# Six buffers for the high parts of g and four for the low parts, where it was four and six

## The chip, the cores and the metric

The kernel runs on one core of one Trainium2 chip. The metric is the time of one execution on the device in microseconds (us), as the median of several runs. A profile comes from one further execution, whose own time is given beside its span.

## The reference

```python
def reference(x, w_in, w_out, w_gate, w1, w2):         # x: 8 x 3072 x 256
    X = fft(fft(x, axis=1), axis=2).real                # 24576 rows of 256
    h = X.reshape(24576, 256) @ w_in                    # 256 -> 2048
    g = h * clip(h + 3, 0, 6) / 6
    x = g @ w_out                                       # 2048 -> 256
    e = argmax(x @ w_gate, axis=1)                      # 8 experts, with the softmax weight of the best
    return weight[e] * (relu(x @ w1[e]) @ w2[e])        # rows grouped by expert
```

## The kernel before

The work has two stages. The first, up to about 2080 us of the span, makes the Fourier transform, the layer with g and the routing; the second runs the experts. The change is in the first. There the tokens of a batch are cut into six chunks of 512 columns, and each chunk is worked through in 8 steps (48 steps a batch, 384 in all), one step for each 256 of the 2048 hidden features.

For accuracy a float32 number is carried as the sum of two parts, a high one in a narrower type and a low one (the remainder), and a product is three matmuls: high with high, high with low, low with high. A step `s` of the loop `step` does this:

- TensorE: 14 matmuls into a tile `ab` of PSUM (`mm1`; called U here), which needs `ab` to be free. There are two `ab` tiles, so U of step s needs that the last reader of `ab` of step s-2 is done.
- `h_of`: ScalarE copies half of `ab` to `A` (L502), VectorE makes a difference (L189) and a sum (L186) in `ab`.
- `relu6`: ScalarE writes two tiles `r` (L508). `gate_h`: VectorE multiplies each with `ab` in place (L515). These two are called the gates here; the second frees `ab`.
- ScalarE copies the two `r` to `gh`, the high part (L962); GpSimd (POOL) subtracts, `gl = r - gh` (L189 on POOL), which also frees `r`.
- Three steps later (`LAG = 3`) TensorE multiplies both with `w_out`: 24 matmuls into `acc` (`mm2`), first 16 that read `gh`, then 8 that read `gl`. That frees `gh` and `gl`.

So `r`, `gh` and `gl` are rings, with two tiles for each step. Their depth is the table `BUFS`, which `halves` reads:

```python
    def halves(tag, dt, s):
        return [pw.tile([P, 2, 256], dt, tag=tag, bufs=BUFS[tag], name=f"{tag}{s}_{n}") for n in range(2)]
```

Between the steps stand other jobs, which are hung on numbered steps: the folds of the next batch (VectorE L186 and L194 on tiles `R` and `H`, POOL on `H`), their splits into parts (ScalarE L182, VectorE L183 on `SC0s`, `SS0s`, `SC`, `SS1s`), the Fourier matmuls (`f`, `fe`, `fo`) with `vc`, `pf` and `pq`, and at each chunk's end the evacuation of `acc` (`xo`, `xp`) and the routing (`rt_...`), with four indirect DMAs that POOL issues to write rows to DRAM (`xs`, L149).

What an engine does in which order is settled when the kernel is built: a scheduler takes instructions by priority (their order in the program) as soon as it holds their inputs to be there and a buffer of their ring to be free. After that each engine runs its own list in that order, and semaphores make it wait.

Of the kernel before, what the change touches and what calls it, by code (L numbers as in the profile page):

```python
# [43 lines left out]
EC = 5  # L44
EX = 6
RKW = 4
BUFS = dict(r=4, gh=4, gl=6)
EXTRA = 23
LATE = (0, 0, 1, 1, 2, 3, 3, 4, 5, 5, 6, 6, 7, 7, 8, 8, 8, 9)
RK = 2  # L50
# [24 lines left out]
def tile_fft_moe(ctx, tc, xr, xf, xcoef, w_in, w_out, w_gate, w1, w2, tabs, fm, misc, tri, sgn8, dstc, maskc, out):  # L75
# [435 lines left out]
    def halves(tag, dt, s):  # L511
        return [pw.tile([P, 2, 256], dt, tag=tag, bufs=BUFS[tag], name=f"{tag}{s}_{n}") for n in range(2)]

# [100 lines left out]
    if True:  # L614
# [409 lines left out]
        ge = pw.tile([P, NTILE, NE + 1], F32, tag="xp", name="ge")  # L1024
        tt = pw.tile([P, NTILE, NE], F32, tag="r", bufs=BUFS["r"], name="tt")
        dve.memset(ge[:, :, 0:1], 1.0)
# [258 lines left out]
```

## Time and profile before

| | us |
|---|---|
| median of 3 runs | 3274.42 |
| lowest and highest | 3268.84, 3277.36 |
| profiled execution, its own time | 3273.91 |
| its span | 3272.1 |

The span is what the profile covers, from the first instruction to the last; the 1.8 us beside it are outside the program's instructions. The time of an engine that counts as busy is not the time that it bounds: TensorE is busy for 95% of the span, and what it waits for is in the rows below.

### The profile page before, as it was taken

How to read it: one execution, taken by the hardware profiler on the slowest of the kernel's cores; microseconds unless marked ns; L12 is line 12 of the kernel's file. 1: busy time of each engine (PE TensorE's matmuls, PEld its weight loads, DVE VectorE, ACT ScalarE, POOL GpSimd, SP SyncE). 2: the span in 40 equal slices, each digit the busy share in tenths (PEclk: the TensorE clock that was granted, in tenths of full speed). 3: DMA queues.
4: the chain of work that ended last, by engine and by line, in shares of the span. 5: the costliest groups of instructions: out<-in, count | busy, mean ns of one | idle time of the engine just before them, and what ended most of it. 6: DMA issues, size and time to landing. Idle time of an engine off the chain costs nothing.

```text
span 3272.1 us, 61901 instructions
## 1 busy us (share of the span) xinstructions
PE 3116.5 (95%) x23482; PEld 2983.7 (91%) x23482; DVE 2117.7 (65%) x3699; ACT 1952.4 (60%) x3339; POOL 2123.1 (65%) x1784
## 2 busy tenths in 40 slices
PE   5899999999999999999999999999999999999998
PEld 5889999999999999999999999988888888888887
DVE  8586777777777777777777666755555555555553
ACT  3566666666666666667666766654444454444453
POOL 5466766766766766766766665676666566666664
PEclk8899999999999999999999999999999999999999
DMA  5100100100100100100100002274555455555550
GB/s 184 62 27 16 44 24 16 43 24 16 44 24 16 44 24 16 44 24 16 34 14 16 15 14 53 63 200 149 147 154 152 140 166 152 149 147 155 145 173 26
DMA packets 256189, 243.14 MB, mean 74 GB/s; under 512 B 157739, under 2 KB 219020, under 8 KB 255888
## 3 DMA queue, kind: packets, MB, share of 16 engines
q1 hardware_dynamic: 234640, 184.66, 20.0%
q0 software_dynamic: 21248, 54.48, 4.6%
q8 instruction: 187, 3.06, 0.4%
q14 instruction: 114, 0.93, 0.1%
HBM read 159.71 MB, written 54.04 MB: 65 GB/s over the span
## 4 chain that ended last, share of the span: by engine, by line
PE 61%; DVE 22%; ACT 10%; issue 3%; POOL 2%; DMA 1%; SPq 0%; ACTq 0%; DVEq 0%; POOLq 0%
PE op L164 16%; PE acc L164 16%; PE hp L164 15%; PE ab L164 11%; DVE r L515 6%; ACT r L508 5%; DVE ab L186 3%; DVE ab L189 3%; ACT xp L546 1%; ACT gh L962 1%; DVE H L194 1%; ACT xo L539 1%; PE wi L164 1%; DVE H L186 1%; DVE xTa L189 1%
## 5 line engine op out<-in xcount | busy, mean ns | idle before, releaser
L189 POOL TENSOR_TENSOR gl<-r,gh 128x512 fp32r<-128x512 f32 x768 | 1018.7, 1349 | 541.4 <-ACT gh L962 536.7
L164 PE MATMUL acc<-WO,gh 128*128 128x264 f32 x6144 | 831.7, 286 | 4.5 <-ACT xo L539 2.3
L515 DVE SCALAR_TENSOR_TENSOR r<-r,ab 128x512 f32<-128x512 f32 x768 | 493.0, 683 | 460.8 <-ACT r L508 452.9
L164 PEld LDWEIGHTS acc<-WO,gh 128*128 128x128 f32 x6144 | 780.9, 190 | 6.5 <-ACT WO L182 3.3
L508 ACT ACTIVATE r<-ab,half 128x512 f32<-128x512 f32 x768 | 486.2, 684 | 241.0 <-DVE ab L186 219.5
L962 ACT ACTIVATE gh<-r 128x512 fp32r<-128x512 f32 x768 | 454.5, 628 | 203.2 <-PE acc L164 145.6
L1000 DVE SCALAR_TENSOR_TENSOR WB<-hp,WA 128x512 fp32r<-128x512 f32 (+1 forms) x472 | 278.7, 607 | 299.4 <-ACT WA L999 293.8
L164 PE MATMUL ab<-pq,WA 128*128 128x256 f32 x2304 | 398.3, 289 | 69.4 <-DVE r L515 63.6
L164 PE MATMUL acc<-WO,gl 128*128 128x264 f32 x3072 | 439.9, 285 | 0.0
L164 PEld LDWEIGHTS ab<-pq,WA 128*128 128x128 f32 x2304 | 330.6, 192 | 90.0 <-issue 82.4
L164 PEld LDWEIGHTS acc<-WO,gl 128*128 128x128 f32 x3072 | 402.8, 189 | 0.0
L999 ACT ACTIVATE WA<-hp 128x512 fp32r<-128x512 f32 (+1 forms) x472 | 241.4, 531 | 194.8 <-PE hp L164 192.7
L164 PE MATMUL ab<-pq,WB 128*128 128x256 f32 x2304 | 342.3, 285 | 0.0
L502 ACT ACTIVATE A<-ab 128x512 f32<-128x512 f32 x384 | 230.1, 599 | 158.7 <-PE ab L164 138.6
L149 POOL DMA_INDIRECT out_dram<-yo,dst x200 | 217.6, 1088 | 156.5 <-DVE yo L1100 119.4
L164 PEld LDWEIGHTS ab<-pq,WB 128*128 128x128 f32 x2304 | 307.7, 193 | 0.0
L164 PE MATMUL hp<-xTb,TB 128*128 128x512 f32 (+1 forms) x1344 | 277.3, 364 | 13.7 <-DVE WB L1000 13.5
L189 DVE TENSOR_TENSOR ab<-A,ab 128x512 f32<-128x512 f32 x384 | 264.7, 689 | 32.8 <-ACT A L502 25.3
L164 PEld LDWEIGHTS hp<-xTb,TB 128*128 128x128 f32 x1344 | 225.8, 188 | 57.9 <-DVE WB L1000 15.2
L164 PE MATMUL hp<-xTa,W1b 128*128 128x512 f32 (+1 forms) x1392 | 275.6, 357 | 1.6 <-DVE WB L1000 1.6
L164 PE MATMUL op<-W2b,WA 128*128 128x256 f32 x1536 | 275.0, 281 | 0.0
L186 DVE TENSOR_TENSOR ab<-A,ab 128x512 f32<-128x512 f32 x384 | 266.8, 695 | 11.5
(269 smaller groups left out, 5300.8 us busy)
## 6 DMA issues: line engine op xcount, KB each, us to landing
w1a<-in_w_dram SPq DMA_DIRECT2D x29, 1024.0 KB
w1b<-in_w_dram SPq DMA_DIRECT2D x29, 1024.0 KB
w2b<-in_w_dram SPq DMA_DIRECT2D x58, 512.0 KB
R<-in_xr_dram SPq DMA_DIRECT2D x32, 774.0 KB
w2a<-in_w_dram SPq DMA_DIRECT2D x29, 768.0 KB
w2d<-in_w_dram SPq DMA_DIRECT2D x28, 256.0 KB
q<-pq SPq DMA_DIRECT2D x288, 1.0 KB
raw<-in_w_in_dram SPq DMA_DIRECT2D x8, 512.0 KB
```

Of the source, the lines that this page charges most:

```text
L149: i = pool.indirect_dma_start(oob_is_err=False, **kw)
L164: i = pe.matmul(*a, **kw)
L186: pinned(eng.tensor_tensor(out=o, in0=a, in1=b, op=ALU.add))
L189: i = eng.tensor_tensor(out=o, in0=a, in1=b, op=ALU.subtract)
L194: pinned(dve.scalar_tensor_tensor(out=o, in0=a, scalar=s, in1=b, op0=ALU.mult, op1=ALU.add))
L502: act.activation(A, h[0], AF.Copy)
L508: act.activation(r, h, AF.Relu, bias=half, scale=1.0 / 6.0)
L515: dve.scalar_tensor_tensor(out=g, in0=r, scalar=1.0, in1=h, op0=ALU.min, op1=ALU.mult)
L539: act.activation(xo[:, t, :], acc[t][:, 0:GW], AF.Copy)
L962: act.activation(gh[n], r[n], AF.Copy)
L999: act.activation(hi, ps, AF.Relu)
L1000: dve.scalar_tensor_tensor(out=lo, in0=ps, scalar=0.0, in1=hi, op0=ALU.max, op1=ALU.subtract)
```

## The change

The depth of two rings is exchanged. `gh` has tiles for three steps instead of two, `gl` for two instead of three. Tiles of both kinds are equally large (512 numbers of 4 bytes on each of 128 partitions), so that the memory is the same.

```diff
-BUFS = dict(r=4, gh=4, gl=6)
+BUFS = dict(r=4, gh=6, gl=4)
```

No instruction of the computation is added or removed. Two things follow for the lists of the engines. An instruction that writes `gh` of step s waits for TensorE's readers of `gh` of step s-3 instead of s-2, and one that writes `gl` of step s for the readers of `gl` of step s-2 instead of s-3. And the scheduler, which held ScalarE's `gh` back until a ring tile was free, places it earlier, and orders other instructions around it anew. From the third batch to the sixth the new order is the same in every batch.

Two places in a batch are shown. The first is POOL's list in a chunk's third step, at the place that the rows below show between 1478 and 1502 us (names with numbers are buffers of one step: `gl_0_19129` and `gl_1_19130` are the two low parts of the step whose U runs just before 1478 us).

```order
 L269 DMA sgn_18889<-in_sgn_dram 128x258
 L578 COPY rt_occ_19373<-cnt 128x8
+L189 TENSOR_TENSOR gl_0_19129<-r_0_19125,gh_0_19127 128x512
+L189 TENSOR_TENSOR gl_1_19130<-r_1_19126,gh_1_19128 128x512
 L149 DMA xs_dram<-xp_18589,pic_19162 198656x260 x3
 L581 TENSOR_TENSOR rt_occ_19373<-rt_occ_19373,rt_ohc_19309 128x8
 L149 DMA xs_dram<-xp_18589,pic_19162 198656x260
-L189 TENSOR_TENSOR gl_0_19129<-r_0_19125,gh_0_19127 128x512
-L189 TENSOR_TENSOR gl_1_19130<-r_1_19126,gh_1_19128 128x512
 L581 TENSOR_TENSOR rt_occ_19373<-rt_occ_19373,rt_ohc_19309 128x8 x2
 L581 TENSOR_TENSOR cnt<-rt_occ_19373,rt_ohc_19309 128x8
```

The two `gl` have moved from behind the four DMA issues to before them.

The second place is ScalarE's list, one chunk earlier in its batch, around 1680 us of the rows below. `r_0_21893` belongs to the step whose U ends before 1678 us, `ab_21939` and `ab_22011` are the tiles of the two steps after it (U at 1683.22 and 1686.53 us). Before:

```order
L508 ACTIVATE r_1_21894<-ab_21833,half 128x512
L539 ACTIVATE xo_21907<-acc_2_21404 128x264
L539 ACTIVATE xo_21907<-acc_3_21405 128x264
L326 ACTIVATE vc_2_0_21915<-f_2_0_21873 128x256
L546 ACTIVATE xp_21908<-xo_21907 128x4x256 x2
L182 ACTIVATE pq_2_21872<-pf_2_0_21916 128x512
L561 ACTIVATE rt_exc_22009<-rt_dc_22006 128x32
L502 ACTIVATE A_21982<-ab_21939 128x512
L962 ACTIVATE gh_0_21895<-r_0_21893 128x512
L962 ACTIVATE gh_1_21896<-r_1_21894 128x512
L508 ACTIVATE r_0_21986<-ab_21939,half 128x512
```

And after the change:

```order
L539 ACTIVATE xo_21907<-acc_3_21405 128x264
L546 ACTIVATE xp_21908<-xo_21907 128x4x256
L962 ACTIVATE gh_0_21895<-r_0_21893 128x512
L962 ACTIVATE gh_1_21896<-r_1_21894 128x512
L546 ACTIVATE xp_21908<-xo_21907 128x4x256
L326 ACTIVATE vc_2_0_21915<-f_2_0_21873 128x256
L502 ACTIVATE A_21982<-ab_21939 128x512
L561 ACTIVATE rt_exc_22009<-rt_dc_22006 128x32
L182 ACTIVATE pq_2_21872<-pf_2_0_21916 128x512
L502 ACTIVATE A_22050<-ab_22011 128x512
L508 ACTIVATE r_0_21986<-ab_21939,half 128x512
```

The two `gh` now stand between the two halves of `xp`, `vc` has moved behind both halves, and `r` of the step at 1683.22 us comes after `A` of the step at 1686.53 us.

## Rows read from the trace of the kernel before

**Rows 1.** The profile's page: busy time of the engines, share of the span, instructions.

```profile
PE 3116.5 (95%) x23482; PEld 2983.7 (91%) x23482; DVE 2117.7 (65%) x3699; ACT 1952.4 (60%) x3339; POOL 2123.1 (65%) x1784
```

**Rows 2.** Busy time by stretch: busy us (instructions) of PE, PEld, DVE, ACT, POOL; PEclk; DMA.

```profile
210.00:2080.00 1870.00, 1810.49 (x14736) 1783.68 (x14735) 1337.28 (x2486) 1279.81 (x2318) 1262.95 (x1256) 0.99 0.08 26
```

**Rows 3.** TensorE's waits from 210 to 2080 us: total, times, longest.

```profile
PE ab L164 <- DVE r L515: 56.7, 55, 2.4
```

**Rows 4.** Timeline of an undisturbed stretch: start, length, engine, [idle before, releaser].

```profile
1303.33 1.15 ACT L962 ACTIVATE gh<-r 128x512 fp32r<-128x512 f32 x2 [0.86 <-PE acc L164]
...
1303.61 1.15 PE L164 MATMUL acc<-WO,gl 128*128 128x264 f32 x8
1304.04 2.54 POOL L189 TENSOR_TENSOR gl<-r,gh 128x512 fp32r<-128x512 f32 x2 [2.02 <-ACT gh L962]
...
1308.60 2.54 POOL L189 TENSOR_TENSOR gl<-r,gh 128x512 fp32r<-128x512 f32 x2 [2.02 <-ACT gh L962]
...
1309.26 1.27 ACT L508 ACTIVATE r<-ab,half 128x512 f32<-128x512 f32 x2 [0.22 <-DVE ab L186]
```

**Rows 5.** VectorE from 1502 to 1747 us by form: count, busy us, mean ns.

```profile
L189 DVE TENSOR_TENSOR ab<-A,ab 128x512 f32<-128x512 f32 x49 | 33.7, 688 | 1.1 <-ACT A L502 0.6
...
L566 DVE SCALAR_TENSOR_TENSOR rt_kc<-rt_dc,iom 128x32 f32<-128x32 f32 x6 | 1.1, 184 | 0.0
```

**Rows 6.** Timeline from 1478 to 1502 us, TensorE, VectorE and POOL.

```profile
1488.05 0.52 PE L164 MATMUL ab<-pq,WA 128*128 128x256 f32 x3
...
1494.18 0.59 PE L164 MATMUL ab<-pq,WA 128*128 128x256 f32 x3 [1.41 <-DVE r L515]
...
1501.40 0.60 PE L164 MATMUL ab<-pq,WA 128*128 128x256 f32 x3 [2.42 <-DVE r L515]
...
1478.49 1.29 DVE L515 SCALAR_TENSOR_TENSOR r<-r,ab 128x512 f32<-128x512 f32 x2 [1.63 <-ACT r L508]
...
1482.02 0.69 DVE L183 SCALAR_TENSOR_TENSOR pq<-pf,pq 128x512 fp32r<-128x512 f32 x1
...
1485.45 1.28 DVE L515 SCALAR_TENSOR_TENSOR r<-r,ab 128x512 f32<-128x512 f32 x2 [0.56 <-issue]
1486.65 3.03 DVE L183 SCALAR_TENSOR_TENSOR SC<-H,SC 128x258 fp32r<-128x258 f32 x2
1489.61 0.42 DVE L186 TENSOR_TENSOR H<-H 128x258 f32<-128x258 f32 x1
...
1492.75 1.28 DVE L515 SCALAR_TENSOR_TENSOR r<-r,ab 128x512 f32<-128x512 f32 x2 [1.40 <-ACT r L508]
...
1481.47 1.03 POOL L149 DMA_INDIRECT xs_dram<-xp,pic  x1 [1.55 <-DVE rt_kc L566]
...
1486.49 2.56 POOL L189 TENSOR_TENSOR gl<-r,gh 128x512 fp32r<-128x512 f32 x2
```

**Rows 7.** Timeline from 1678 to 1699 us, all four engines.

```profile
1691.09 0.52 PE L164 MATMUL ab<-pq,WA 128*128 128x256 f32 x3
...
1697.74 0.59 PE L164 MATMUL ab<-pq,WA 128*128 128x256 f32 x3 [1.92 <-DVE r L515]
...
1682.43 2.05 ACT L546 ACTIVATE xp<-xo 128x1024 uint16<-128x1024 uint16 x2
...
1682.99 0.42 DVE L327 TENSOR_TENSOR pf<-f,vc 128x256 f32<-128x256 f32 x1
...
1688.82 1.28 DVE L515 SCALAR_TENSOR_TENSOR r<-r,ab 128x512 f32<-128x512 f32 x2 [1.11 <-ACT r L508]
1690.03 3.55 DVE L183 SCALAR_TENSOR_TENSOR SC0s<-H,SC0s 128x258 fp32r<-128x258 f32 x1
...
1689.45 2.55 POOL L189 TENSOR_TENSOR gl<-r,gh 128x512 fp32r<-128x512 f32 x2
...
1692.55 1.29 POOL L189 TENSOR_TENSOR H<-R 128x258 f32<-128x258 f32 x2
```

**Rows 8.** POOL's instructions that write gl: who waited for them (us, times).

```profile
  ACT r L508: 5.7, 11
```

## The prediction

> **What bounds the kernel now.** I read the page first, then the busy time of the first stage, then TensorE's waits in it, and last the places where those waits stand. The page shows TensorE busy for 95% of the span [rows 1]. From 210 to 2080 us, nearly all of the stage that the change touches, it is busy for 1810 of 1870 us at a granted clock of 0.99, while VectorE, ScalarE and POOL are each busy for some 70% [rows 2]. So a shorter wait of another engine gives nothing, unless TensorE stood behind it. It stands behind one thing in the main: 56.7 us in 55 waits of a U for VectorE's gates, that is, for an `ab` tile [rows 3]. That is the most the change can give back there, 1.7% of the time.
>
> TensorE never waits for `gh` or `gl` in these rows. What waits for the rings is ScalarE: in an undisturbed stretch `gh` waits 0.86 us until TensorE has read the `gh` of two steps before, and `gl` on POOL follows it [rows 4]. This is the wait that the change removes, and it lies beside TensorE's work: a step lasts 4.56 us there (from one `gl` to the next), and no U waits.
>
> **The change in an undisturbed step.** `gh` no longer waits, which gains nothing in the end. `gl` now waits for TensorE's readers of `gl` two steps before. These are the 8 matmuls at 1303.61; the sixth is the last that reads the first tile. At 1.15 us for eight it ends about 1304.5, where `gl` started at 1304.04 [rows 4]: `gl` comes some 0.45 us later in each step. Behind it on POOL stand folds and scatters, and ScalarE's `r` of two steps later waits for its tile. That `r` starts at 1309.26 and `gl` ended at 1304.04 + 2.54 = 1306.58, so that 2.7 us of slack become 2.2. Cost nothing, as long as POOL is not more than 2.2 us late.
>
> **The change where TensorE stands.** The waits come in a pattern that each of six batches repeats. Two places carry most of it: 1.92 us around 1698 [rows 7], and 1.41 and 2.42 us around 1494 and 1501 [rows 6]; six times 5.75 is 34.5 of the 56.7 us. In both, one thing lengthens VectorE's list ahead of the gates. At 1690.03 the low part of `SC0s` takes 3.55 us, of which 0.42 are its work (the like instruction on as many numbers at 1489.61). It ends only when POOL, which runs `gl` and then `H` without a gap from 1689.45, is past its third instruction [rows 7]. At 1486.65 the two `SC` take 3.03 us while POOL runs `gl` from 1486.49 to 1489.05 [rows 6]. VectorE instructions with two inputs in SBUF wait there for POOL's.
>
> The Trainium skill (SBUF — State Buffer, Who interferes with whom) says that a VectorE instruction with two SBUF inputs contends with a GpSimd instruction that reads SBUF, and that the one which comes first holds the ports for its whole length. The rows agree that it waits, but 3.55 us is longer than the one instruction of POOL (1.28 us, half of 2.55) that the rule lets it wait for. By the rule a collision that stays would cost 1.3 us at most, and the lower bound around 1690 below would be a gain of 0.5 instead of a loss of 0.4.
>
> The changed order moves POOL's `gl` ahead of the scatters at both places (shown for one), so that POOL issues scatters while VectorE does its splits. A scatter does not hold VectorE up: `pq`, with two SBUF inputs, took its usual 0.69 us at 1482.02 beside the scatter of 1481.47 to 1482.50 [rows 6]. Against that, ScalarE's list puts `gh` between the halves of `xp` and `vc` behind them, and VectorE's copy into `xp` and `pf` wait for both. So the gates come later before they come sooner.
>
> *Around 1690.* `xp` ended at 1682.43 + 2.05 = 1684.5; two `gh` of 1.15 us together [rows 4] put it near 1685.4 (`vc` no longer ahead of it), `vc` at 1685.8. On VectorE follow two `pf` of 0.42, then a difference and a sum for each of two steps and one `pq`, five of 0.69, some ten routing operations of 0.18 [rows 5, 7], partly overlapped (1.3 to 1.8), and the gates, 1.28: 1685.8 + 0.8 + 3.5 + 1.6 + 1.3 = 1693.0, against 1690.1 now. The U at 1691.09 has six matmuls of 0.12 us (the step has 38 in 4.56 us) moved ahead of it, so it could start at 1691.8 and waits 1.3 us, until 1693.1. The next gates need `SC0s` at 0.42 and 1.28 more, 1694.8. The U after that starts when TensorE gets there, 14 + 18 matmuls or 3.85 us on, at 1697.0 where it was 1697.74. I take a gain of 0.5 us. With `SC0s` at 3.55 again it is 1698.1, a loss of 0.4; with nothing late, 1696.4, a gain of 1.4.
>
> *Around 1494.* Here the two `gh` can start when the gates of their step end, 1479.8, and stand before both halves of `xp`: 1.15 + 2.05 + 0.4 for `vc` is 1483.3, and the same 7.2 us of VectorE's list put the first gates' end at 1490.5 where it was 1486.7 [rows 6], and the U of 1488.05 (seven matmuls ahead of it, so 1488.9) at 1490.6. But the sum and difference of the next step now stand before these gates, and the `SC` pair is beside scatters: 0.8 us instead of 3.03, `H` 0.4, gates 1.3: next gates end at 1493.0, where it was 1494.0. That U starts at 1494.4, 31 matmuls on and no longer waiting. From its gates to the next ones VectorE needed 1501.25 - 1494.03 = 7.2 us; from 1493.0 that is 1500.2 at the latest. The U of 1501.40 starts near 1500.1: a gain of 1.35. If `SC` takes 3.03 again the gates end 1495.2 and this U starts at 1502.4, a loss of 1.0; if the later pair of splits and `H` (1.5 us at 1495.73) are freed too, TensorE's own pace allows 1498.9, a gain of 2.5.
>
> **The sum.** 6 x 1.35 + 6 x 0.5 = 11.1 us. The smaller waits (56.7 - 34.5 = 22 us) and the first two hundred us, where the order changes as well, I take at nothing: the lists move both ways there, and they may give or take some 8 us. Bounds of the two places: 6 x (-1.0 - 0.4) = -8 and 6 x (2.5 + 1.4) = +23. Against the profiled execution's 3273.9 us (its span and 1.8 us beside it; 0.5 us below the median of the runs, so no correction) that gives 3262.8. About 0.3%, 10 us, is what a measurement here can tell from no change.
>
> **The rivals.**
> - *Gain given back.* The later gates at the chunk ends eat what the splits give, and the undisturbed steps stay at TensorE's pace: 3274. For it speaks that TensorE is at 1810 of 1870 us already; against it, that POOL's and VectorE's collision is 3.1 us at one place.
> - *Slower: POOL late, `r` held.* Four scatters of 1.0 us at a chunk's end put POOL behind, and `gl` may no longer run ahead of TensorE by three steps. Then `r` waits for `gl`, the gates for `r` and U for the gates. It decides when `gl` is more than 2.2 us late. Before, `r` waited so for only 5.7 us, 11 times [rows 8], which speaks against it. Price: 0.45 us at each of 48 chunk ends, 22 us, less the 11: 3285.
> - *More freed.* If the collisions go at all places, half of the 56.7 us comes back: 3273.9 - 28.3 = 3245.6. That each collision is chance speaks against it: every `gl` moves by 0.45 us against the folds `R` and `H` in each step, so that new collisions come with those that go.
>
> **How the numbers follow.** Forecast 45% (3262.8, itself 3255 to 3270; six in ten of it faster by more than 0.3%, the rest the same), given back 23% (nearly all the same), slower 18%, more freed 14%. That makes faster 0.43, same 0.36, slower 0.21. The range takes the better half of the last case and the slower one but for its tail: 3243 to 3284.
>
> **What would show it.** Right: TensorE's waits for the gates fall by about ten us; the wait at the place of 1698 is gone and one of 1 to 2 us stands a step earlier; `SC0s` there takes 0.4 us; ScalarE's `gh` hardly waits for TensorE and POOL's `gl` waits for TensorE instead of ScalarE. Wrong: `SC0s` and `SC` as long as before, or moved collisions at folds that were free; ScalarE's `r` waiting for POOL for tens of us; new waits for the gates in the third and fifth step of the chunks.

## The result and the profile after

The changed kernel takes 3296.1 us (median of 6 runs, 3292.2 to 3302.2) where the kernel before took 3274.0 beside it: a ratio of 1.0073, 95% interval 1.0061 to 1.0085, so 22 us slower. The forecast was 3262.8, 11 us faster, in a range from 3243 to 3284.

The profile's page, busy time of the engines as in [rows 1], has nothing of this: each engine does what it did before.

```profile
PE 3117.0 (95%) x23482; PEld 2983.1 (91%) x23482; DVE 2123.4 (64%) x3699; ACT 1958.9 (59%) x3339; POOL 2118.6 (64%) x1784
```

The stretch of [rows 2] again, by busy time: TensorE 1789.6 us where it was 1810.5, 21 us less work in the same time.

```profile
210.00:2080.00 1870.00, 1789.58 (x14536) 1761.10 (x14535) 1323.28 (x2454) 1267.38 (x2281) 1239.94 (x1241) 0.99 0.08 26
```

TensorE's waits in it, as in [rows 3]: the wait for the gates grew from 56.7 us to 63.4, and more stand behind the routing (`rt_kc`, 0.6 us before, and `rt_mc`) and the evacuation (`xo`), for which no wait is listed before.

```profile
PE ab L164 <- DVE r L515: 63.4, 67, 3.0
PE ab L164 <- DVE rt_kc L592: 4.5, 7, 3.3
PE acc L164 <- ACT xo L539: 4.3, 8, 1.4
PE ab L164 <- DVE rt_mc L558: 3.5, 12, 0.3
```

POOL's `gl` in the same stretch, what it waited for and, below, who waited for it, which answers to [rows 8]:

```profile
  PE acc L164: 393.8, 176
  ACT gh L962: 99.0, 59
...
  ACT r L508: 36.3, 44
```

So `gl` did change from waiting for `gh` to waiting for TensorE, and ScalarE's `r` waits for `gl` six times as long as before (36.3 us, before 5.7). That looks like the rival "POOL late, `r` held". The experiments show that it isn't.

**Where the 21 us between the two spans arise.** Each step has one `A` on ScalarE, and the starts of the first `A` of each piece, in either trace, cut the stage (us; "what follows" ends with POOL's last instruction; the runs below stand beside the two for later use):

| kernel | step 0 to 80 | five batches, 80 to 320 | 320 to 383 | what follows |
|---|---|---|---|---|
| before | 475.5 | 1228.9 | 322.7 | 1184.8 |
| changed | 471.1 | 1234.2 | 341.8 | 1185.3 |
| gl two steps, gh two | 469.4 | 1226.5 | 322.6 | 1184.9 |
| changed, gh behind A everywhere | 473.2 | 1220.1 | 328.3 | 1185.6 |
| changed, gh behind A from step 328 | 474.0 | 1233.6 | 327.9 | 1183.7 |
| changed, gh behind A at chunk ends up to 327 | 458.9 | 1204.2 | 343.9 | 1186.6 |
| both of these | 465.1 | 1203.8 | 329.3 | 1187.7 |
| gh behind A at all chunk ends, A behind gh elsewhere | 473.4 | 1235.4 | 338.3 | 1182.9 |

The start gains 4.5 us, the five batches lose 5.3, and 19.2 us are lost in the last eight chunks: 0.6 in the first of them, where the last folds and splits stand, and the rest in the seven after it, which have none. The prediction had looked at none of these chunks.

**The last chunks.** Busy time from 1800 to 1965 us, first of the kernel before:

```profile
1800.00:1965.00 165.00, 165.00 (x1362) 163.90 (x1360) 100.45 (x201) 112.24 (x203) 103.38 (x102) 0.99 0.04 14
```

and of the changed kernel:

```profile
1800.00:1965.00 165.00, 155.47 (x1264) 152.91 (x1263) 102.77 (x196) 108.41 (x196) 99.97 (x99) 0.99 0.04 14
```

TensorE was never idle there; now it does 98 matmuls fewer (11.9 us, at 0.121 us apart) and is idle for 9.5, at the same granted clock, 0.99. These 9.5 us are waits that the profile lists, 5.2 of them for the gates; the other 2.4, by difference, are starts that come a little late, as shown below. The timeline of an undisturbed step of the changed kernel, which answers to [rows 4], shows one of two causes (start, length, engine, idle before):

```profile
1837.44 0.52 PE L164 MATMUL ab<-pq,WA 128*128 128x256 f32 x3
...
1841.46 0.63 ACT L962 ACTIVATE gh<-r 128x512 fp32r<-128x512 f32 x1 [0.81 <-DVE r L515]
1842.00 0.58 ACT L502 ACTIVATE A<-ab 128x512 f32<-128x512 f32 x1
1842.11 0.59 PE L164 MATMUL ab<-pq,WA 128*128 128x256 f32 x3
1842.17 2.55 POOL L189 TENSOR_TENSOR gl<-r,gh 128x512 fp32r<-128x512 f32 x2 [2.11 <-PE acc L164]
...
1842.61 0.70 DVE L189 TENSOR_TENSOR ab<-A,ab 128x512 f32<-128x512 f32 x1 [0.65 <-ACT A L502]
1843.34 0.69 DVE L186 TENSOR_TENSOR ab<-A,ab 128x512 f32<-128x512 f32 x1
1844.13 1.27 ACT L508 ACTIVATE r<-ab,half 128x512 f32<-128x512 f32 x2 [1.03 <-DVE ab L186]
1845.43 1.28 DVE L515 SCALAR_TENSOR_TENSOR r<-r,ab 128x512 f32<-128x512 f32 x2 [1.40 <-ACT r L508]
1846.21 0.63 ACT L962 ACTIVATE gh<-r 128x512 fp32r<-128x512 f32 x1 [0.81 <-PE acc L164]
1846.75 0.58 ACT L502 ACTIVATE A<-ab 128x512 f32<-128x512 f32 x1
```

The first `gh` of a step now stands ahead of the next step's `A` in ScalarE's list. The U that writes that `A`'s input begins at 1837.44, and its 14 matmuls are over by 1839.26, but `A` starts at 1842.00, right behind `gh`. And `gh` needs the gate, the gate `r`, `r` the sum, the sum the difference and the difference the `A` before: the rows close a loop, 0.61 + 0.73 + 0.79 + 1.30 + 0.78 + 0.54 = 4.75 us from one `A` to the next, where TensorE's work takes 4.57. (For the `gh` at 1846.21 the row names TensorE. But TensorE's 16 matmuls that had to be done for it had started at 1839.10 and took 2.09 us, while the first of the two gates ended at 1846.12: it is the gate.) That ScalarE doesn't let a ready `A` pass a waiting `gh` is what the Trainium skill says (PSUM — Partial Sum Buffer, Engine vs sequencer instructions: its queue is strictly first in, first out); the rows agree, since `A` waits 2.7 us with its input there. In the kernel before, `A` of the next step stood ahead of `gh` in these steps, and no loop closed.

TensorE's share of this doesn't appear among its waits: the records of its matmuls last 0.28 us (their ends are modelled) and start every 0.12, so that a start that is late by up to 0.16 us leaves no idle time between two records. The first two matmuls of the U at 1842.11 start 0.22 and 0.19 us after the ones ahead of them, instead of 0.12.

**The chunk's end.** The place of [rows 7] in the changed kernel, 1686 to 1699 us:

```profile
1685.87 1.06 ACT L546 ACTIVATE xp<-xo 128x1024 uint16<-128x1024 uint16 x1
...
1686.84 1.14 ACT L962 ACTIVATE gh<-r 128x512 fp32r<-128x512 f32 x2
1687.02 0.60 PE L164 MATMUL ab<-pq,WA 128*128 128x256 f32 x3
1687.88 1.04 ACT L546 ACTIVATE xp<-xo 128x1024 uint16<-128x1024 uint16 x1
1688.83 0.36 ACT L326 ACTIVATE vc<-f 128x256 f32<-128x256 f32 x1
1688.95 0.17 DVE L605 COPY xp<-dst_sb 128x12 f32<-128x12 f32 x1 [1.75 <-ACT xp L546]
1690.41 2.99 POOL L189 TENSOR_TENSOR gl<-r,gh 128x512 fp32r<-128x512 f32 x2 [3.93 <-PE acc L164]
1690.68 1.57 DVE L183 SCALAR_TENSOR_TENSOR pq<-pf,pq 128x512 fp32r<-128x512 f32 x1
1692.17 1.28 DVE L595 TENSOR_TENSOR rt_kc<-rt_kc,rt_ohc 128x32 f32<-128x32 f32 x1
1693.37 0.68 DVE L186 TENSOR_TENSOR ab<-A,ab 128x512 f32<-128x512 f32 x1
1697.83 0.42 DVE L183 SCALAR_TENSOR_TENSOR SC0s<-H,SC0s 128x258 fp32r<-128x258 f32 x1
1698.06 0.59 PE L164 MATMUL ab<-pq,WA 128*128 128x256 f32 x3 [2.28 <-DVE r L515]
```

`SC0s` has its 0.42 us, as predicted. But the two `gh` between the halves of `xp` keep `vc` back, and VectorE stands with its copy into `xp` for 1.75 us. So `pq` comes just when `gl` runs: it takes 1.57 us, and `rt_kc` with its 32 numbers 1.28. The sum behind them is late, the gates too, and U waits 2.28 us. VectorE's instructions from 500 to 1755 us by form in the changed kernel (count, then busy us and mean ns) show the exchange:

```profile
L183 DVE SCALAR_TENSOR_TENSOR pq<-pf,pq 128x512 fp32r<-128x512 f32 x21 | 29.5, 1405 | 0.5
L595 DVE TENSOR_TENSOR rt_kc<-rt_kc,rt_ohc 128x32 f32<-128x32 f32 x31 | 22.8, 735 | 0.0
L183 DVE SCALAR_TENSOR_TENSOR SC<-H,SC 128x254 fp32r<-128x254 f32 x11 | 8.3, 758 | 0.0
L183 DVE SCALAR_TENSOR_TENSOR SC0s<-H,SC0s 128x258 fp32r<-128x258 f32 x11 | 7.5, 679 | 0.0
L183 DVE SCALAR_TENSOR_TENSOR SC<-H,SC 128x258 fp32r<-128x258 f32 x11 | 4.6, 421 | 0.0
L194 DVE SCALAR_TENSOR_TENSOR H<-H 128x258 f32<-128x258 f32 x11 | 4.6, 419 | 0.0
L183 DVE SCALAR_TENSOR_TENSOR SS1s<-H,SS1s 128x254 fp32r<-128x254 f32 x11 | 4.5, 413 | 0.0
```

against the kernel before:

```profile
L183 DVE SCALAR_TENSOR_TENSOR SC0s<-H,SC0s 128x258 fp32r<-128x258 f32 x11 | 20.3, 1842 | 0.0
L183 DVE SCALAR_TENSOR_TENSOR SC<-H,SC 128x258 fp32r<-128x258 f32 x11 | 15.8, 1436 | 0.0
L183 DVE SCALAR_TENSOR_TENSOR pq<-pf,pq 128x512 fp32r<-128x512 f32 x20 | 13.8, 690 | 1.2
L183 DVE SCALAR_TENSOR_TENSOR SS1s<-H,SS1s 128x254 fp32r<-128x254 f32 x11 | 11.2, 1017 | 0.0
L194 DVE SCALAR_TENSOR_TENSOR H<-H 128x258 f32<-128x258 f32 x11 | 11.2, 1014 | 0.0
L595 DVE TENSOR_TENSOR rt_kc<-rt_kc,rt_ohc 128x32 f32<-128x32 f32 x30 | 9.8, 326 | 0.0
L183 DVE SCALAR_TENSOR_TENSOR SC<-H,SC 128x254 fp32r<-128x254 f32 x11 | 6.8, 622 | 0.0
```

The splits `SC0s` and `SC` gave back 22.5 us, the split `SS1s` and the fold `H` another 13.3; `pq` and `rt_kc` took 28.7, with one instruction more of each in the window. So in sum these instructions of VectorE take no longer than before. What counts is where the time goes, and `pq` and the routing stand at the chunks' ends, ahead of gates that a U waits for.

### The profile page after: what moved, and what is told of

Its sections match the earlier page's. It is cut to its first block, busy times and chain, and to the rows that moved or that the text cites. A ratio compares the mean times of both kernels' runs of the same rounds, so it can differ in the third digit from the quotient of the medians.

```text
span 3293.3 us, 62041 instructions
## 1 busy us (share of the span) xinstructions
PE 3117.0 (95%) x23482; PEld 2983.1 (91%) x23482; DVE 2123.4 (64%) x3699; ACT 1958.9 (59%) x3339; POOL 2118.6 (64%) x1784
## 4 chain that ended last, share of the span: by engine, by line
PE 47%; DVE 28%; ACT 16%; issue 3%; POOL 3%; DMA 1%; SPq 0%; ACTq 0%; DVEq 0%; POOLq 0%
PE op L164 16%; PE hp L164 15%; PE acc L164 8%; ACT r L508 8%; DVE r L515 8%; PE ab L164 6%; DVE ab L186 5%; DVE ab L189 4%; ACT gh L962 2%; ACT xp L546 2%; POOL gl L189 1%; DVE pq L183 1%; DVE R L194 1%; DVE rt_kc L595 1%; PE wi L164 1%
## 5 line engine op out<-in xcount | busy, mean ns | idle before, releaser
L164 PE MATMUL acc<-WO,gh 128*128 128x264 f32 x6144 | 844.1, 287 | 7.2 <-ACT xo L539 6.5
L164 PEld LDWEIGHTS acc<-WO,gh 128*128 128x128 f32 x6144 | 788.9, 191 | 9.9 <-ACT xo L539 8.4
L962 ACT ACTIVATE gh<-r 128x512 fp32r<-128x512 f32 x768 | 466.8, 631 | 106.1 <-DVE r L515 103.4
L164 PE MATMUL hp<-xTb,TB 128*128 128x512 f32 (+1 forms) x1344 | 277.4, 364 | 13.3 <-DVE WB L1000 13.0
```

Source lines behind the costliest of these rows:

```text
L164: i = pe.matmul(*a, **kw)
L962: act.activation(gh[n], r[n], AF.Copy)
```

## The experiments

Theory A: the loss lies in the lists that the deeper `gh` makes the scheduler write. Theory B: it lies in the ring of `gl` that is one step shorter.

**Half of the change alone.** Only `gl` is made shorter.

```diff
-BUFS = dict(r=4, gh=4, gl=6)
+BUFS = dict(r=4, gh=4, gl=4)
```

> gh keeps its two steps, and gl goes from three to two, so half of the change: no deeper gh. The lists of TensorE, ScalarE and VectorE are then the same as before, row for row, and POOL's nearly so. Theory A (the loss lies in the new lists: ScalarE has gh of a step ahead of A of the next step, and between the halves of xp): no loss, 3274 us within 6. Theory B (the loss lies in the two-step ring of gl: POOL's gl waits for TensorE, r for gl, the gates for r): most of the loss is there, 3288 to 3297.

Measured: 3266.5 us, ratio 0.9986 (0.9976 to 0.9996). No loss, with the lists of ScalarE and VectorE the same as before, row for row. `gl` waits 310.1 us for TensorE, and ScalarE's `r` 26.0 us for `gl`, and with these lists that doesn't make the kernel slower: theory B falls. The 5 us below the kernel before are within the 0.3%.

**The rings of the change, the old place of gh.** What writes `gh` and `gl` is emitted one step later, behind the next step's `A`, with an edge that fixes the order of `A` and `gh` in ScalarE's list and makes nobody wait. The scheduler orders the rest of all lists around it anew.

```diff
                 h = h_of(ab, s)
+                if "low" in hold:
+                    hold.pop("low")(hold["A"])
...
-                for n in range(2):
-                    act.activation(gh[n], r[n], AF.Copy)
-                for n in range(2):
-                    sub(pool, gl[n], r[n], gh[n])
+                def low(after, r=r, gh=gh, gl=gl):
+                    for n in range(2):
+                        i = act.activation(gh[n], r[n], AF.Copy)
+                        tc.add_manual_dep(i.ins, after.ins.name, NOSYNC, reason="behind A")
+                    for n in range(2):
+                        sub(pool, gl[n], r[n], gh[n])
+                hold["low"] = low
```

> The changed rings (gh six tiles, gl four), but each step's gh is held behind A of the next step in ScalarE's list, as nearly all of them stood before. Theory A: the steps of the last chunks go back from 4.75 to 4.57 us and the time to 3268 to 3280. Theory B: the rings are those of the change, so 3290 to 3298.

Measured: 3263.8 us, 0.9969 (0.9958 to 0.9981): the loss is gone and 10 us beside it, with the rings of the change. `r` waits 48.2 us for `gl` in this run, more than in the changed kernel, so this wait isn't what the 22 us are.

**Both rings deep.** `xp` gives the memory (so do two other tiles that share its ring).

```diff
-BUFS = dict(r=4, gh=6, gl=4)
+BUFS = dict(r=4, gh=6, gl=6)
...
-                xp = pw.tile([P, 4, XW], I32, tag="xp", name=f"xp{z}")
+                xp = pw.tile([P, 4, XW], I32, tag="xp", bufs=1, name=f"xp{z}")
```

> gh has three steps as in the change and gl keeps its three; to make room xp has one buffer instead of two, which is what the next run has alone. Theory A: slower than the next run by 10 to 25 us, because ScalarE's list has gh ahead of A again (in the chunks 42 to 46 in 26 of 40 steps). Theory B: gl is as deep as before, so within 5 us of the next run.

And its baseline, `xp` alone:

> The rings of before, xp with one buffer instead of two: the baseline of the run with both rings deep. Both theories: 3274 within 8, if the rows are out of xp before the next chunk's end; the order changes a little, too.

Measured: 3474.1 and 3443.5 us. The second was off by 170 us for both theories: ScalarE's `xp` stands until the scatters of the `xp` before have landed, in this row of ScalarE's waits from 210 to 2080 us:

```profile
ACT xp L546 <- DMA xs_dram<-xp,pic: 149.2, 41, 5.0
```

Most of that is the order of the kernel itself. It issues the scatters of a chunk only at the next chunk's end: an `xp` written until 1519.9 us is scattered from 1557.1 to 1562.3, and the next one starts at 1564.8, after ScalarE has waited 4.0 us. A scatter takes some 2.7 us there from its issue to its landing.

The deeper `gh` costs 31 us in this pair, with `gl` as deep as it was. The sign is that of theory A, but with a baseline so changed the pair proves little.

**The place in the stage.** The edge of the second run, but only in some steps; where it isn't, `gh` is emitted as in the changed kernel. In the last chunks:

```diff
+                if s >= 328:
+                    hold["low"] = low
+                else:
+                    low(None)
```

> The changed kernel, with gh held behind A of the next step only from step 328 on (the chunks 41 to 47); up to there its lists are the changed kernel's, row for row. Theory A, with most of the loss in the last chunks (17 of 21 us by the times of A): 3276 to 3283. If the loss came from the whole stage in equal parts: 3292 to 3296.

> As the run before, but gh is held only in the steps 2 to 4 of each of those chunks, where the evacuation, xp and the routing stand. By the widths between one A and the next, a chunk of the changed kernel loses 4.0 us: 0.8 in four undisturbed steps of 4.75 instead of 4.57 us, 3.2 in the other four. Theory A1 (the chunk's end carries the loss: gh between the halves of xp, r behind two A): 12 of the 17 us come back, 3282 to 3287. Theory A2 (the loop A, difference, sum, r, gate, gh, A of the undisturbed steps makes both): 3290 to 3295.

> The complement: gh is held behind A from step 328 on in all steps but 2 to 4 of a chunk. Theory A1: only the 0.19 us of each undisturbed step come back, 4 to 6 us in all, 3289 to 3293. Theory A2: most of the 17, 3278 to 3284.

Measured: 3281.7 us, 1.0025 (1.0016 to 1.0034); 3287.9, 1.0045 (1.0031 to 1.0058); 3284.4, 1.0040 (1.0026 to 1.0054). The last chunks give back 14.5 of the 22 us; the chunk's ends alone 8, the undisturbed steps alone 12. Together that is more than both at once, and both times lie between what A1 and A2 gave, so neither holds alone: the loop and the chunk's end seem to help make the same waits. The 14.5 us aren't all of the loss there: with the edge the last eight chunks take 327.9 us, 5.2 more than in the kernel before, and no run shows why.

**The lists with the old rings.**

```diff
-BUFS = dict(r=4, gh=6, gl=4)
+BUFS = dict(r=4, gh=4, gl=6)
```

> The rings of before (gh four tiles, gl six) with gh held behind A in every step, as in the run that took 3263.8 us with the changed rings. If the lists alone set the time: 3261 to 3268. If the deeper gh is what that run gained by: 3271 to 3277.

Measured: 3262.5 us, 0.9970 (0.9958 to 0.9982), the same as with the rings of the change. With lists that are mostly but not wholly the same, the depth of either ring does nothing that can be told. `r` waits 40.3 us for `gl` here, with `gl` as deep as before: with this edge, then, that wait doesn't come from the shorter ring.

**The chunk's ends in the batches, and more of the loop.** First the edge in `s < 328 and s % STEPS in (2, 3, 4)` alone; then the opposite edge, `A` behind the first `gh` of the step before, in all steps but 3 to 5:

```diff
+        if "gh0" in hold and s % STEPS not in (3, 4, 5):
+            tc.add_manual_dep(i.ins, hold["gh0"].ins.name, NOSYNC, reason="behind gh")
```

> The changed kernel, with gh held behind A of the next step only up to step 327 and only in the steps 2 to 4 of a chunk; from step 328 on the lists of the changed kernel stand. In the changed kernel a batch takes about 247 us (245.6 before, 244.0 with gh behind A everywhere), with new TensorE waits of 1.8 and 2.3 us behind pq and rt_kc on VectorE. Theory A (gh at the chunk's end, between the halves of xp, makes those): the batches go to 244 to 245 us and the time to 3278 to 3288. If the batches' loss has another place: 3292 to 3298.

> The dose doubled: the changed kernel, with A held behind the first gh of the step before in every chunk of the stage, in all steps but 3 to 5, where the changed kernel's list has it so mainly in the last chunks. Theory A (a loop A, difference, sum, r, gate, gh, A of 4.75 us where TensorE needs 4.57): the undisturbed steps of all chunks take 4.75 us, up to 0.19 us in 5 steps of 39 more chunks, and the time is 3318 to 3336. If that order is harmless by itself: 3290 to 3300.

> gh held behind A everywhere, gh and gl of two steps each, and r of three steps instead of two. r can no longer be held up by gl of two steps before, for which ScalarE waited 36 us in the changed kernel and 48 us in the run with gh behind A. If that wait costs nothing (theory A): 3259 to 3267, as with the other rings and the same lists. If it costs (theory B): under 3256.

Measured: 3257.9 us, 0.9961 (0.9947 to 0.9975); 3304.7, 1.0095 (1.0078 to 1.0111); 3256.1, 0.9953 (0.9939 to 0.9968). The first gives back 38 us where 8 to 18 were expected: a batch goes from 247 to 241 us. The second has its undisturbed steps at 4.7 to 4.8 us in all chunks, as expected, and yet costs only 9 us more than the changed kernel: a miss. The third, with `r` a step deeper, has no such wait of `r` for `gl` any more, and ScalarE's and VectorE's lists are those of the run with the old rings, row for row. It lies at the bound that theory B gave (under 3256). The 6.4 us between the two are not clear of noise, as their intervals overlap; so that wait of `r` may cost up to some such amount, but not the 22 us.

**What these left open.** Which `gh` at the chunk's end, and why the loop cost so little.

The edge of the second run stands again only in some steps: in the first of these `if s >= 328 or s % STEPS in (2, 3, 4)`, in the second `if s < 328 and s % STEPS == 2`, in the third `if s < 328 and s % STEPS in (3, 4)`. The fourth has it `if s % STEPS in (2, 3, 4)`, and the opposite edge in all other steps.

> The changed rings, with gh held behind A of the next step in the steps 2 to 4 of every chunk, and from step 328 on in all steps. The two parts alone took 3257.9 us and 3281.7 us, against 3296 for the changed kernel: if they add, 38 and 14.5 us come back, 3240 to 3248. If the second part is worth less once the first is in: 3250 to 3257.

> The changed kernel, with gh held behind A only in step 2 of a chunk, the step of the evacuation, and only up to step 327. Its lists for TensorE, VectorE and POOL are then those of the run that held steps 2 to 4, but for four rows. If the gh between the halves of xp is what costs in the batches: 3255 to 3262, as that run (3257.9). If the gh of steps 3 and 4 and the r behind two A carry it: 3285 to 3296.

> The complement: gh held behind A only in the steps 3 and 4 of a chunk, up to step 327. The lists of TensorE, VectorE and POOL are the changed kernel's but for two rows. If the gh of step 2 is the cause in the batches: 3291 to 3298, no gain. If steps 3 and 4 carry it: 3258 to 3275.

> gh behind A in the steps 2 to 4 of every chunk, and A behind the first gh of the step before in all others: the loop by itself, with the chunk's ends in order. Against the first run of this call. If the loop costs its 0.19 us in four steps of each of 46 chunks: 35 us above that run, 3275 to 3285. If the loop costs little wherever other work fills the chunk: under 3265.

Measured: 3245.6 us, 0.9909 (0.9893 to 0.9926); 3262.1, 0.9967 (0.9955 to 0.9979); 3301.2, 1.0084 (1.0069 to 1.0098); 3295.6, 1.0068 (1.0050 to 1.0085).

Step 2 alone gives 34 of the 38 us, steps 3 and 4 alone none (5 us slower than the changed kernel, and above what was expected). The place of the rows from 1686 to 1698 us in the run with step 2 alone, between 1652 and 1663 us (its line numbers are a little higher):

```profile
1652.82 2.04 ACT L547 ACTIVATE xp<-xo 128x1024 uint16<-128x1024 uint16 x2
1654.43 0.59 PE L165 MATMUL ab<-pq,WA 128*128 128x256 f32 x3
1654.71 0.42 ACT L327 ACTIVATE vc<-f 128x256 f32<-128x256 f32 x1
1656.05 0.20 DVE L596 TENSOR_TENSOR rt_kc<-rt_kc,rt_ohc 128x32 f32<-128x32 f32 x1
1656.81 0.69 DVE L184 SCALAR_TENSOR_TENSOR pq<-pf,pq 128x512 fp32r<-128x512 f32 x1
1657.68 2.54 POOL L190 TENSOR_TENSOR gl<-r,gh 128x512 fp32r<-128x512 f32 x2 [2.12 <-ACT gh L968]
1662.51 0.59 PE L165 MATMUL ab<-pq,WA 128*128 128x256 f32 x3 [0.27 <-DVE r L516]
```

`vc` starts 0.28 us after U where it was 1.81; `pq` is done before `gl` begins, and U's wait of 2.28 us is 0.27. The one edge lets the scheduler move other instructions too: POOL's four folds `H`, which ran behind this `gl` from 1693.37 us, run ahead of it from 1653.43. So the 34 us are those of the edge with all that it moves, not of the two `gh` by themselves.

With the chunk's ends in order the loop costs 50 us (3295.6 against 3245.6; 35 were expected: a miss), in the five batches 31.7. Against the run with `gh` behind `A` in every step (3263.8) it costs 32, near the 35 of the sum; the rest is a gain of the run that it was set against, told at the end of this section. So the loop isn't cheap. Why it cost so little in the run with the opposite edge alone was not tried: perhaps the chunk's end made TensorE wait anyway there, and a slower run-up only shortened that wait.

The parts add: 38 and 14.5 us off the changed kernel would be 3243.6, and 3245.6 was measured, 0.9% under the kernel before. TensorE's wait for the gates, from 210 us to the end of the stage, is then 39.0 us:

```profile
PE ab L165 <- DVE r L516: 39.0, 70, 2.1
```

The deeper `gh` may have a share in this. With the edge in every step, in the second run, the five batches take 1220.1 us, and 1203.8 where `gh` may go ahead in the undisturbed steps of the batches. It does so in 30 of their 240 steps; in the kernel before, with two steps of `gh`, it goes ahead in none of these steps. If that is the reason, the ring's third step is worth some 16 us by the lists that it allows, once the chunk's end is out of its reach. But these edges were not run with the old rings, so that is not shown; nor is why a `gh` that goes ahead should gain in the batches, while it loses in the last chunks.

## Why the prediction was wrong

**The two places: right in kind, and near in sum.** From the third batch to the sixth, TensorE's waits at the three U of [rows 6, 7] were 5.95 us a batch and are 3.63: a gain of 14 us over six batches where 11.1 were forecast. Around 1494, 4.04 us became 1.36 (2.7 gained, forecast 1.35, bound 2.5); around 1690, 1.91 became 2.27 a step earlier (0.4 lost, forecast 0.5 gained, bound 0.4 lost), and not because `SC0s` collided again but because `pq` and `rt_kc` did. That the sum of the two places is near is in part luck, then: one gained twice its forecast, the other lost. By the working's own steps the gain around 1494 is 1.05 rather than 1.35, too, as the gates' end goes from 1501.25 to 1500.2. The `SC` pair takes 0.75 us beside a scatter at 1492.55, as forecast.

**The step that failed: "The smaller waits ... and the first two hundred us ... I take at nothing".** The waits elsewhere in a batch grew from 2.8 to 6.2 us, 20 us over six batches where some 8 either way were allowed for, with 1.81 us at a single place (the sixth step of the batch's second chunk) where 0.12 stood. The one at that place has the cause that the prediction saw and priced only at the two places it looked at, the `gh` that stands between the halves of `xp`: it is gone in the run with the edge in step 2 alone. For the others that is not shown. Around 1690 the prediction took the two `gh` as a delay of 1.2 us for what follows, and then added up VectorE's instructions at their undisturbed lengths; it didn't ask what POOL does at that time. `gl`, which now waits for TensorE, starts when the late `pq` does.

**The larger step that failed: an undisturbed step at "Cost nothing, as long as POOL is not more than 2.2 us late".** That was worked out on an undisturbed step of the batches, where `A` mostly still stands ahead of `gh`, and only from the waits of `gl` and `r`; where `gh` would stand in ScalarE's list there was not asked. In the last chunks the scheduler, with a free `gh` buffer, wrote `gh` first in 38 of the 64 steps, where it had been 2. There an undisturbed step takes 4.75 us instead of 4.57, and the last eight chunks 19.2 us more, of which the edge that puts `gh` back behind `A` returns 13.9. The sum multiplied two places by six, and the last chunks' list was not read.

**The rival with the right price had the wrong cause.** "Slower: POOL late, `r` held" was priced at 22 us by 0.45 us at each of 48 chunk ends, and with the 11 of the gain taken off its time was 3285, 11 us under what was measured. `r` does wait for `gl`, 36.3 us; but it waits 26.0 us in the run without a loss and 48.2 in one that is faster. That the 22 us are also the loss is chance, and only the runs could tell.

**The Trainium skill's rule** (SBUF — State Buffer, Who interferes with whom) would have a VectorE instruction with two SBUF inputs wait out one GpSimd instruction. `rt_kc`, of 0.19 us, took 1.28 beside a `gl` of 1.29 us for each half in undisturbed steps: here the row agrees with the rule, where `SC0s` in the kernel before did not. The prediction read that row short: between the rows of POOL that it shows stands a fourth instruction.

```profile
1691.94 0.66 POOL L186 TENSOR_TENSOR H<-R 128x258 f32<-128x258 f32 x1
```

`SC0s` ends at 1693.58, so its own 0.42 us begin at 1693.16, when the two `gl` (until 1692.00), this `H` (until 1692.60) and the first half of the next pair, whose two take 1.29, are over or all but over: it stood behind four of them, not three.

## What to carry to other kernels

Where a scheduler orders the engines, a ring's depth isn't only a matter of waiting: the full ring was what kept `gh` behind work that mattered more, and the deeper ring let it go ahead. Read the new lists in every kind of stretch, the last one too, and look in each engine's list for an instruction (here the next `A`) that stands behind the end (here `gh`) of a chain which the same instruction of the step before began: that closes a loop, and a step can't be shorter than it. When depth lets work run early that others must not wait for, fix its place with an order edge: such edges, with what else the scheduler then moved, took 50 us off the changed kernel here, 28 of them off the kernel before.

## What the runs showed of the hardware

A VectorE instruction on 32 numbers a partition takes 1.28 us instead of 0.19 when a POOL instruction with SBUF inputs runs, and such collisions move rather than vanish when the order changes (35.8 us less at the splits and `H`, 28.7 more at `pq` and `rt_kc`). Behind instructions of POOL that follow one another without a gap a VectorE instruction can wait for more than one: 3.55 us instead of 0.42 behind four. TensorE can lose 0.19 us in each step without a wait of its own in the profile, because the records of its matmuls overlap by 0.16 us: the starts of the matmuls show it, the idle time doesn't. And a buffer that a scatter reads is free only when the scatter has landed, 2.7 us after its issue: with one `xp` instead of two, and scatters issued a chunk later, ScalarE waited 149.2 us, and the kernel took 169 us more.
